# Weight decoding without GpSimd's add, one fp32 matmul in place of a split pair, and a new order for block 0

## The chip, the cores and the metric

The kernel runs on one core of a Trainium2 chip. A core has TensorE (PE), with its weight loads listed apart as PEld, VectorE (DVE), ScalarE (ACT), GpSimd (POOL) and SyncE (SP), which issues the transfers. The metric is the device time of one execution in microseconds (us), the median of several runs.

## The reference

Three stages follow one another, all in float32 (shapes in the comments).

```python
# 1. local + global attention, 4 batches x 8 heads, 512 local and 32 global positions, head size 64
out_g = softmax(scale * q_g @ k_all.T) @ v_all
out_l = softmax(concat([scale * q_l @ k_g.T, banded(scale * q_l @ k_l.T)])) @ v_all   # band of +-32
x = concat([out_g, out_l]) as (2176 tokens, 512)
# 2. soft mixture of experts, 8 experts x 4 slots
logits = x @ phi;  d = softmax(logits, over tokens);  c = softmax(logits, over slots)
slot_out[e] = relu((d.T @ x)[e] @ w1[e]) @ w2[e]
x = c @ slot_out
# 3. gated feed-forward layer, w_in 512 x 2048, w_out 2048 x 512
h = x @ w_in
out = (h * cos(h)) @ w_out
```

The last layer's weights reach the kernel as 64-bit words (`w_in` and `w_out` seen as int64, which are float64 numbers), so each weight is two 32-bit words, and the kernel makes a float32 of them itself. That is what is called decoding here.

## The kernel before

**Stages.** Attention runs in 40 units (32 with one pair of heads and one half of the positions each, 8 for the global rows), software-pipelined: for every step `s` a string of letters (`ORDER`, with exceptions in `TURN_OF`) names the stages in the order in which they are issued, each for another unit. Then come the experts, and then the feed-forward layer in four blocks of 512 tokens plus one tile of 128 (the global rows). In each block 16 slices `f` of 128 hidden columns are computed: `u_mm` (L1006, h of one slice), `u_round`, `u_frac`, `u_cos`, `u_mul` (the gate: L1012 on ACT, L1019 on DVE, L1026 on ACT, L1031 on DVE), a split into a high part (`u_hi` L1037 on ACT or `u_hi2` L1045 on DVE) and a rest (`u_lo`, L1050), and `o_pass` (L1117), twelve matmuls of 512 columns per slice in three passes of four: high x high, high x low, low x high.

**Order.** Nothing reorders the program: each engine works through its instructions as they are issued, and waits at the first that is not ready. In block 0 the order is the string `SWEEP`, one letter per step; I call the time of this string the sweep. After it, blocks 1 to 3 follow a fixed loop.

**What decoding takes.** For a tile of 128 x 512 weights, `high` (L156, ACT) makes the upper bits from the high word; another ACT instruction (L699 for `w_in`, L972 in `d_low` for `w_out`) makes the bits that come from the low word, a whole number; `shift3` (L151, DVE) shifts the upper bits left by three; `add_low` (L160, POOL) adds the two. `w_in` (16 tiles) is decoded during attention: stage `A` issues the two ACT instructions at the end of a step of the list `DEC`, stage `B` of the next step the shift, stage `C` the add. `w_out` (16 tiles, `f`) is decoded in the sweep, by the letters h, l, s, a. There each tile is then split for the matmul into a rounded high half (`d_h`: letter d on ACT L987, D on DVE L989) and a rest (`d_l`: letter e on DVE, E on POOL, both L993).

**w_in's part.** Before the sweep's slices can start, `w_in` is multiplied with the slot outputs: `cm_mm` (L925, letter 3, four times), then `cm_copy` (L932, letter 4, ACT) and `cm_rest` (L936, letter 8, DVE) split the result into two rounded parts, and `cm_sel` (L943, letter 5) sums the four groups of rows with two matmuls against a 0/1 matrix `sel_r`. The letters 0, 1, 2 do the same for the first 128 columns by a short way, 6 and 7 (L952, L957) split the sum for `u_mm`.

**The tile of global rows** has its own steps in the sweep: M (`x_mm` L1063), n, F, x, U, y or Y, z or Z (L1068 to L1090) and X (`x_out` L1096, three matmuls for each f).

**Buffers that make engines wait for each other.** `u_mm` writes into two PSUM banks in turn, so slice i+2 cannot start before the last reader of slice i (`u_mul` or `u_hi2`) is done. Upper bits, low bits and the joined `w_out` tile have three buffers each (`NC`), those of `w_in` one each, so the next `high` on ACT waits until the tile before is joined.

## Time and profile before

| | us |
|---|---|
| median of 3 runs | 404.56 (403.65 to 406.88) |
| span of the profiled execution | 401.8 |
| PE busy | 381.6 (95% of the span) |
| DVE busy | 274.7 (68%) |
| ACT busy | 226.3 (56%) |
| POOL busy | 211.9 (53%) |

The span runs from the first to the last instruction of one profiled execution; the page gives no other time of that execution, and the median of the runs shown is 2.8 us above this span. In the rows below, a line number is that of the kernel before, "x" a count, "idle before" the time for which the engine stood still ahead of the group, and the name behind `<-` what ended it.

### The profile page before, as it was taken

What the parts mean: (1) busy time and instruction counts of PE and PEld (TensorE: products, weight loads), DVE (VectorE), ACT (ScalarE), POOL (GpSimd) and SP (SyncE); (2) the same over time, 40 slices, a digit from 0 to 9 for tenths busy, and PEclk for the clock granted to TensorE, in tenths of its full rate; (3) what the DMA queues carried; (4) which work ended last, traced back from release to release, by engine and by line L of the source; (5) the groups of instructions that cost most, each with busy time, mean ns of one, the idle gap of its engine ahead of it and who ended that gap; (6) DMA issues with size and microseconds to landing.
All of it is one profiled execution on the core that took longest, in us unless ns stands there. A gap on an engine that the chain in (4) does not pass through costs nothing.

```text
span 401.8 us, 10160 instructions
## 1 busy us (share of the span) xinstructions
PE 381.6 (95%) x3922; PEld 287.2 (71%) x3922; DVE 274.7 (68%) x793; ACT 226.3 (56%) x462; POOL 211.9 (53%) x265
## 2 busy tenths in 40 slices
PE   7998989988989899999999899999999999999996
PEld 6777867766767543335677677888888888888885
DVE  5699788779859632138999988655556565665561
ACT  3488788778878313359888764433433433533430
POOL 0879879858862000026989796234434434354441
PEclk9999999999999999999999999999999999999999
DMA  7999999976859899999100000300002000110002
GB/s 260 366 364 409 406 411 409 403 264 249 285 181 342 310 374 409 409 408 409 75 0 0 2 0 1 132 1 1 2 0 106 0 1 2 44 60 2 0 0 106
DMA packets 23519, 72.36 MB, mean 180 GB/s; under 512 B 3120, under 2 KB 3888, under 8 KB 23472
## 3 DMA queue, kind: packets, MB, share of 16 engines
q1 hardware_dynamic: 23472, 71.72, 47.1%
...
## 4 chain that ended last, share of the span: by engine, by line
PE 76%; ACT 9%; DVE 7%; DMA 4%; issue 3%; SPq 1%; POOL 0%; DVEq 0%; ACTq 0%; POOLq 0%
PE bank L1117 38%; PE bank L306 6%; PE bank L861 4%; PE bank L826 4%; PE bank L351 3%; PE bank L1006 3%; PE bank L324 3%; DMA big<-in_w_out 3%; PE bank L419 2%; PE bank L451 2%; PE bank L443 2%; ACT sml L330 2%; PE bank L1096 2%; DMA big<-in_kq 2%; ACT sml L434 1%
## 5 line engine op out<-in xcount | busy, mean ns | idle before, releaser
L1050 POOL TENSOR_TENSOR big<-sml,sml 128x512 fp32r<-128x512 f32 x58 | 76.7, 1323 | 83.8 <-DVE sml L1039 73.3
L1117 PE MATMUL bank<-big,sml 128*128 128x512 f32 (+1 forms) x442 | 109.6, 382 | 0.4 <-DVE big L993 0.4
L1117 PEld LDWEIGHTS bank<-big,sml 128*128 128x128 f32 x442 | 81.2, 189 | 18.3 <-DVE big L993 0.9
L1012 ACT ACTIVATE sml<-bank 128x512 int32<-128x512 f32 x63 | 37.6, 596 | 87.7 <-PE bank L1006 87.5
L160 POOL TENSOR_TENSOR sml<-sml,sml 128x512 int32<-128x512 int32 x32 | 43.7, 1366 | 57.6 <-ACT sml L972 50.8
L1117 PE MATMUL bank<-big,big 128*128 128x512 f32 (+1 forms) x221 | 59.5, 381 | 0.0
L133 POOL TENSOR_SCALAR sml<-wide 64x258 f32<-64x258 f32 (+2 forms) x94 | 48.1, 511 | 15.1 <-PE bank L351 4.4
L1117 PEld LDWEIGHTS bank<-big,big 128*128 128x128 f32 x221 | 40.9, 188 | 8.6
L306 PEld LDWEIGHTS bank<-big,sml 128*64 128x64 f32 x672 | 34.8, 140 | 8.8 <-issue 5.4
L1019 DVE SCALAR_TENSOR_TENSOR sml<-sml,bank 128x512 f32<-128x512 int32 x32 | 21.9, 684 | 26.6 <-ACT sml L1012 26.6
L1019 DVE SCALAR_TENSOR_TENSOR wide<-sml,bank 128x512 f32<-128x512 int32 x32 | 22.0, 686 | 26.2 <-ACT sml L1012 26.0
L306 PE MATMUL bank<-big,sml 128*64 128x128 f32 (+2 forms) x672 | 38.7, 262 | 1.0 <-issue 1.0
L316 DVE CUSTOM_DVE_ANT_0 sml<-bank,mk 128x128 f32<-128x128 f32 x128 | 29.4, 286 | 8.4 <-PE bank L306 8.1
L133 POOL TENSOR_SCALAR sml<-big 64x32 f32<-64x32 f32 (+1 forms) x62 | 23.6, 381 | 14.8 <-PE bank L306 5.8
L318 DVE TENSOR_TENSOR sml<-sml,mx 128x512 f32<-128x512 f32 x32 | 26.7, 835 | 1.1
L1006 PE MATMUL bank<-big,sml 96*128 96x512 f32 x60 | 24.3, 405 | 1.5 <-DVE sml L1045 1.5
L351 PE MATMUL bank<-sml,sml 128*32 128x65 f32 x640 | 21.4, 223 | 4.1 <-ACT sml L330 3.4
L1117 PE MATMUL bank<-wide,sml 128*128 128x512 f32 (+1 forms) x102 | 24.8, 383 | 0.2 <-ACT sml L1037 0.2
L330 ACT ACTIVATE sml<-bank 128x512 f32<-128x512 f32 x32 | 18.9, 591 | 9.6 <-PE bank L324 9.3
L151 DVE TENSOR_SCALAR sml<-sml 128x512 int32<-128x512 int32 x32 | 22.3, 698 | 2.0 <-ACT sml L156 2.0
L1039 DVE CAST sml<-sml 128x512 fp32r<-128x512 f32 x46 | 20.3, 441 | 4.6
L1026 ACT ACTIVATE sml<-wide 128x512 f32<-128x512 f32 x32 | 20.0, 625 | 5.3 <-DVE wide L1019 5.3
...
## 6 DMA issues: line engine op xcount, KB each, us to landing
...
```

What stands on the lines that cost most here:

```text
L133: pool.tensor_scalar(out=out, in0=in_, scalar1=1.0, scalar2=0.0, op0=ALU.mult, op1=ALU.add)
L160: add.tensor_tensor(out=out.bitcast(I32), in0=ci, in1=r.bitcast(I32), op=ALU.add)
L306: pe.matmul(o, lhs, rhs, start=True, stop=True)
L316: dve.tensor_tensor_reduce(out=ss[:, g], in0=s[:, g], in1=mk[:, MASK[4 * key[3] + g]], op0=ALU.add, op1=ALU.max, scale=1.0, scalar=-3.0e38 ...
L318: dve.tensor_tensor(out=ss, in0=ss, in1=mx.to_broadcast([128, 4, 128]), op=ALU.subtract)
L330: act.activation(out=pt, in_=TT.pop(key), func=AF.Exp, scale=SCALE)
L351: pe.matmul(o[32 * qd:32 * qd + 32, i2, 65 * h:65 * h + 65], pt[:, c8 // 2, l0:l0 + 32], vt[:, HD * h:HD * h + HD + 1], start=True, stop=True)
L1006: pe.matmul(UU[s][:, 0:n], wcs[f], ctb[bi][0:96, 0:n].bitcast(F32R), start=True, stop=True)
L1012: act.activation(out=AA[s][:, 0:n], in_=UU[s][:, 0:n], func=AF.Copy, bias=0.25)
L1019: dve.scalar_tensor_tensor(out=FR[s][:, 0:n], in0=AA.pop(s)[:, 0:n], scalar=0.25, in1=UU[s][:, 0:n], op0=ALU.subtract, op1=ALU.subtract)
L1050: eng.tensor_tensor(out=gl[:, 0:n], in0=GG.pop(s)[:, 0:n], in1=GH[s][:, 0:n].bitcast(F32), op=ALU.subtract)
L1117: pe.matmul(acc[j][:, 0:c1 - c0], g, whl[f][k == 1][:, c0:c1], start=(f == 0 and k == 0), stop=(f == NFF - 1 and k == 2))
```

## The change

Both words are now joined by one VectorE instruction: ACT's instruction for the low word is scaled and offset so that its whole number lies within three bits, and `join` shifts the upper bits and ORs the low ones in. `shift3`, `add_low` and stage `C` of the attention's order go away, and with them letter s; letter a is now the join on DVE. `cm_sel` is a single matmul on unrounded float32 numbers, so `cm_rest` (letter 8) and the rounded copy of the 0/1 matrix go away. The string `SWEEP` is new. It does the same work with 16 letters s and 4 letters 8 less, and also moves some work between engines: d on ACT 14 to 7, D on DVE 2 to 9, E on POOL 13 to 6, e on DVE 3 to 10, u_hi on ACT (g) 8 to 13, u_hi2 on DVE (G) 10 to 5, v on POOL 12 to 11, V on DVE 6 to 7, R on DVE 1 to 0 and r on ACT 18 to 19, Y on DVE 2 to 1 and y on ACT 2 to 3.

```diff
-    def shift3(c):
-        ci = c.bitcast(I32)
-        dve.tensor_scalar(out=ci, in0=ci, scalar1=3, scalar2=None, op0=ALU.logical_shift_left)
-    def add_low(c, r, out, add):
-        ci = c.bitcast(I32)
-        add.tensor_tensor(out=out.bitcast(I32), in0=ci, in1=r.bitcast(I32), op=ALU.add)
+    def low(raw, r):
+        act.activation(out=r.bitcast(I32), in_=words(raw)[0].bitcast(U32), func=AF.Copy, scale=0.9 * 2.0 ** -29, bias=0.29)
+
+    def join(c, r, out):
+        dve.scalar_tensor_tensor(out=out.bitcast(I32), in0=c.bitcast(I32), scalar=3, in1=r.bitcast(I32),
+                                 op0=ALU.logical_shift_left, op1=ALU.bitwise_or)
...
-            act.activation(out=r.bitcast(I32), in_=words(raw)[0].bitcast(U32), func=AF.Copy, scale=2.0 ** -29)
+            low(raw, r)
...
             dc, n, raw, c, r = dpend.popleft()
-            shift3(c)
-            dadd.append((dc, n, c, r))
+            wi[dc, n] = smalls.popleft()
+            join(c, r, wi[dc, n])
...
-    def dec_c():
-        if dadd:
-            dc, n, c, r = dadd.popleft()
-            wi[dc, n] = smalls.popleft()
-            add_low(c, r, wi[dc, n], pool)
...
-        act.activation(out=p1s[n][1][:, c:512].bitcast(F32R), in_=o[:, c:512], func=AF.Copy)
-
-    def cm_rest(n):
-        (o, h, l), c = p1s[n], c0_of(n)
-        dve.tensor_tensor(out=l[:, c:512].bitcast(F32R), in0=o[:, c:512], in1=h[:, c:512], op=ALU.subtract)
+        act.activation(out=t[:, c:512], in_=o[:, c:512], func=AF.Copy)
...
-        for k, t in enumerate((h, l)):
-            pe.matmul(o[0:96, c:512], sel_r, t[:, c:512].bitcast(F32R), start=(k == 0), stop=(k == 1))
-            smalls.append(t)
+        pe.matmul(o[0:96, c:512], sel3, t[:, c:512], start=True, stop=True)
...
-    "h0lsh13ls2m43hraas8hfl4d5836c7434uEm5M8arm8gfvAr6cfhdBCsuE7cgulsm5rvgAfdvancBlmr6euGCFdAfBmx7aDC5Uch6uGyAEsM"
+    "0ll3h1al342Dmh5era34f65d7c3e6ulmM7rGn4fmvhAFcaxCrudBUgfElmVAcrBuhlfCgacYmvAdurBegzhfmClVcAruhCagaBdflm4AecDMVr"
```

**DVE, the start of the sweep.** These are DVE's first instructions in the sweep before (L151 the shifts, L957 letters 2 and 7, L936 letter 8, L1019 the first u_frac, L1031 the first u_mul):

```order
L151 TENSOR_SCALAR sml_2990<-sml_2990 128x512
L151 TENSOR_SCALAR sml_2991<-sml_2991 128x512
L957 SCALAR_TENSOR_TENSOR big_3037<-bank_74,big_3037 32x128
L151 TENSOR_SCALAR sml_2992<-sml_2992 128x512
L936 TENSOR_TENSOR sml_3048<-bank_75,sml_3047 128x384
L1019 SCALAR_TENSOR_TENSOR sml_3001<-sml_2999,bank_71 128x512
L936 TENSOR_TENSOR sml_3064<-bank_76,sml_3063 128x512
L957 SCALAR_TENSOR_TENSOR sml_3075<-bank_77,sml_3075 32x384
L1031 TENSOR_TENSOR sml_3005<-bank_71,big_3003 128x512
```

And now (L155 the join, L939 letters 2 and 7, L968 letter D, L972 letter e, L998 u_frac, L1010 u_mul, L1024 u_hi2):

```order
L155 SCALAR_TENSOR_TENSOR sml_2979<-sml_2973,sml_2976 128x512
L939 SCALAR_TENSOR_TENSOR sml_3023<-bank_74,sml_3023 32x128
L968 CAST big_3034<-sml_2979 128x512
L972 TENSOR_TENSOR big_3034<-sml_2979,big_3034 128x512
L155 SCALAR_TENSOR_TENSOR sml_2980<-sml_2974,sml_2977 128x512
L998 SCALAR_TENSOR_TENSOR sml_2984<-sml_2982,bank_71 128x512
L939 SCALAR_TENSOR_TENSOR sml_3049<-bank_77,sml_3049 32x384
L972 TENSOR_TENSOR wide_3052<-sml_2980,wide_3052 128x512
L1010 TENSOR_TENSOR sml_2988<-bank_71,big_2986 128x512
```

The three shifts and the two L936 ahead of the first u_mul are gone; two joins, a cast and two subtractions stand there instead.

**POOL, the start of the sweep.** Before, with L160 the add, L993 letter E and L1050 u_lo:

```order
L160 TENSOR_TENSOR sml_2996<-sml_2990,sml_2993 128x512
L160 TENSOR_TENSOR sml_2997<-sml_2991,sml_2994 128x512
L993 TENSOR_TENSOR wide_3066<-sml_2996,wide_3066 128x512
L160 TENSOR_TENSOR sml_2998<-sml_2992,sml_2995 128x512
L1050 TENSOR_TENSOR big_3010<-sml_3005,sml_3007 128x512
L993 TENSOR_TENSOR big_3116<-sml_2997,big_3116 128x512
L1050 TENSOR_TENSOR big_3011<-sml_3006,sml_3008 128x512
```

And now (L1029 u_lo, L972 letter E, L1069 letter z):

```order
L1029 TENSOR_TENSOR big_2993<-sml_2988,sml_2990 128x512
L972 TENSOR_TENSOR big_3094<-sml_2981,big_3094 128x512
L1029 TENSOR_TENSOR big_2995<-sml_2988,sml_2992 128x512
L1069 TENSOR_TENSOR big_3001<-big_2999,big_3000 128x512
L972 TENSOR_TENSOR big_3187<-sml_2981,big_3187 128x512
```

POOL has 43 instructions in the sweep before, and 19 now; the adds are gone, in attention (16) too.

## Rows read from the trace of the kernel before

**Rows 1.** Busy time by stretch: attention, experts, sweep, blocks 1 to 3 (columns: PE, PEld, DVE, ACT, POOL).

```profile
10.00:142.00 132.00, 122.11 (x2551) 95.88 (x2551) 107.61 (x505) 98.51 (x228) 91.51 (x169) 1.00 0.90 339
142.00:177.40 35.40, 35.30 (x303) 12.77 (x302) 8.46 (x23) 11.27 (x23) 0.00 (x0) 1.00 1.02 399
177.40:253.60 76.20, 71.55 (x340) 52.77 (x341) 69.32 (x99) 58.87 (x109) 60.00 (x43) 1.00 0.22 85
253.60:401.80 148.20, 144.64 (x669) 119.08 (x668) 83.95 (x146) 54.62 (x98) 59.52 (x46) 1.00 0.08 30
```

**Rows 2.** Chain that ended last, two pieces of block 3 (start us, length us, what).

```profile
347.52 2.79 PE bank L1117 x12
350.54 2.81 PE bank L1117 x15
```

**Rows 3.** Waits of PE in the sweep, the longest (us, times, longest).

```profile
PE bank L1006 <- DVE sml L1045: 1.5, 2, 0.8
```

**Rows 4.** Timeline of DVE, the `u_hi2` of slice 7, for which slice 9 waited.

```profile
212.23 0.67 DVE L1045 TENSOR_TENSOR sml<-bank,sml 128x512 fp32r<-128x512 f32 x1
```

**Rows 5.** Timeline of DVE, five instructions in a row (start, length, operation).

```profile
201.62 1.33 DVE L151 TENSOR_SCALAR sml<-sml 128x512 int32<-128x512 int32 x1
202.88 0.67 DVE L1019 SCALAR_TENSOR_TENSOR sml<-sml,bank 128x512 f32<-128x512 int32 x1
203.47 0.68 DVE L1031 TENSOR_TENSOR sml<-bank,sml 128x512 f32<-128x512 f32 x1
204.08 0.41 DVE L151 TENSOR_SCALAR sml<-sml 128x512 int32<-128x512 int32 x1
204.41 0.67 DVE L1072 SCALAR_TENSOR_TENSOR big<-big,bank 128x512 f32<-128x512 int32 x1
```

**Rows 6.** Timeline of POOL, the instruction that ran while that first shift began.

```profile
201.38 1.29 POOL L1050 TENSOR_TENSOR big<-sml,sml 128x512 fp32r<-128x512 f32 x1
```

**Rows 7.** Groups of DVE's instructions in the sweep (busy us, mean ns, idle before).

```profile
L151 DVE TENSOR_SCALAR sml<-sml 128x512 int32<-128x512 int32 x16 | 13.2, 827 | 1.2 <-ACT sml L156 1.2
...
L1050 DVE TENSOR_TENSOR big<-sml,sml 128x512 fp32r<-128x512 f32 x6 | 5.7, 958 | 0.1
L993 DVE TENSOR_TENSOR big<-sml,big 128x512 fp32r<-128x512 f32 x3 | 4.5, 1505 | 0.4 <-ACT big L987 0.4
...
L1090 DVE TENSOR_TENSOR big<-big,big 128x512 fp32r<-128x512 f32 x2 | 3.0, 1504 | 0.0
...
L989 DVE CAST big<-sml 128x512 fp32r<-128x512 f32 x2 | 2.3, 1150 | 0.0
```

**Rows 8.** The adds among POOL's groups in the sweep.

```profile
L160 POOL TENSOR_TENSOR sml<-sml,sml 128x512 int32<-128x512 int32 x16 | 22.8, 1426 | 52.2 <-ACT sml L972 50.8 <-DVE sml L151 1.4
```

**Rows 9.** Two lines over the whole run (duration ns min/median/max, first and last start).

```profile
L318 DVE TENSOR_TENSOR sml<-sml,mx x32: 691/706/1553, 7.5 to 126.5; 128x512 f32<-128x512 f32 x32
...
L1039 DVE CAST sml<-sml x46: 426/427/1051, 256.1 to 390.3; 128x512 fp32r<-128x512 f32 x46
```

**Rows 10.** Timeline at the sweep's start: DVE's second shift, and PE's first pass of slice 0.

```profile
178.38 1.17 DVE L151 TENSOR_SCALAR sml<-sml 128x512 int32<-128x512 int32 x1 [0.65 <-ACT sml L156]
...
186.09 2.13 PE L1117 MATMUL bank<-wide,sml 128*128 128x512 f32 x8 [0.25 <-ACT sml L1037]
```

**Rows 11.** Chain that ended last, one piece in the expert stage.

```profile
142.21 7.00 PE bank L826 x64
```

**Rows 12.** PE's groups in the sweep by form, the one of cm_sel.

```profile
L943 PE MATMUL bank<-sml,big 128*96 128x512 f32 x6 | 2.0, 408 | 0.5 <-DVE sml L957 0.5
```

**Rows 13.** Waits of weight loads for POOL in attention.

```profile
PEld bank L306 <- POOL sml L133: 2.6, 7, 0.8
```

**Rows 14.** Timeline of DVE, one shift in attention.

```profile
50.30 0.58 DVE L151 TENSOR_SCALAR sml<-sml 128x512 int32<-128x512 int32 x1 [0.84 <-ACT sml L156]
```

**Rows 15.** Groups of DVE's instructions from 10 to 142 us.

```profile
L318 DVE TENSOR_TENSOR sml<-sml,mx 128x512 f32<-128x512 f32 x30 | 25.3, 845 | 1.0
...
L151 DVE TENSOR_SCALAR sml<-sml 128x512 int32<-128x512 int32 x16 | 9.1, 569 | 0.8 <-ACT sml L156 0.8
```

More of the change, by code (lines that the diff above doesn't have):

```diff
@@ L628, in fused_kernel @@
     wid = deque((dc, n) for n in range(4) for dc in range(4))
-    dpend, dadd = deque(), deque()
+    dpend = deque()
     post = deque()
@@ L720, in pump @@
             key, n = wq[0][0], len(wq)
-            load_w(1, spare=1 + len(wid) + len(dpend) + len(dadd))
+            load_w(1, spare=1 + len(wid) + len(dpend))
             if len(wq) == n:
@@ L741, in fused_kernel @@
         "q": lambda s: prep_in(s + 3),
-        "C": lambda s: dec_c(),
         "m": lambda s: prep(s + 1, 1),
@@ L760, in fused_kernel @@
             STAGES[stage](s)
-        if dc_r and not wid and not dpend and not dadd:
+        if dc_r and not wid and not dpend:
             smalls.extend(dc_r.release() + dr_r.release())
@@ L894, in fused_kernel @@
     route_t(1, x_r())
-    sel_r = ctb[4][:, 128:224].bitcast(F32R)
-    dve.tensor_copy(out=sel_r, in_=sel3)
     ex_w2(0, lambda: ex_t(1), MID[0])
@@ L971, in d_low, with d_join @@
         DC[f, 1] = t = r_r()
-        act.activation(out=t.bitcast(I32), in_=words(wt["wo", f])[0].bitcast(U32), func=AF.Copy, scale=2.0 ** -29)
-    def d_shift(f):
-        shift3(DC[f, 0])
-    def d_add(f, eng):
+        low(wt["wo", f], t)
+    def d_join(f):
         DW[f] = wd_r()
-        add_low(DC.pop((f, 0)), DC.pop((f, 1)), DW[f], eng)
+        join(DC.pop((f, 0)), DC.pop((f, 1)), DW[f])
         bigs.append(wt.pop(("wo", f)))
@@ L1174, in fused_kernel @@
     kinds = {
-        "h": (d_hi, None), "l": (d_low, None), "s": (d_shift, None),
-        "a": (d_add, pool), "d": (d_h, act), "D": (d_h, dve), "e": (d_l, dve), "E": (d_l, pool),
+        "h": (d_hi, None), "l": (d_low, None), "a": (d_join, None), "d": (d_h, act), "D": (d_h, dve), "e": (d_l, dve), "E": (d_l, pool),
         "0": (lambda n: cm_dir(), None), "1": (lambda n: cm_hi("d"), None), "2": (lambda n: cm_lo("d"), None),
-        "3": (cm_mm, None), "4": (cm_copy, None), "8": (cm_rest, None), "5": (cm_sel, None), "6": (cm_hi, None), "7": (cm_lo, None),
+        "3": (cm_mm, None), "4": (cm_copy, None), "5": (cm_sel, None), "6": (cm_hi, None), "7": (cm_lo, None),
         "m": (u_mm, None), "r": (u_round, act), "R": (u_round, dve), "f": (u_frac, None), "c": (u_cos, None),
```

14 lines of the change are left out of this document (7 added, 7 removed).

## The prediction, made before the changed kernel ran

> **What bounds the kernel now.** I read the busy time by stretch first [rows 1], to see which stage has room. In blocks 1 to 3 the chain of work shows PE without a hole: two pieces start 3.02 us apart for 13 matmuls of 512 columns, 0.232 us each [rows 2]. No weight is decoded there, so that stretch stays. The experts (142 to 177.4) have PE busy for 35.30 of 35.40 us and stay too. What can move is the sweep, 76.2 us, and attention.
>
> What PE has to do in the sweep, by the program: 180 + 12 matmuls of `o_pass`, 48 of X, 19 `u_mm` and 8 of `cm_sel`, 267 x 0.232 = 61.9 us. The float32 work beside it: four groups of four side-by-side matmuls go at 7.00 us / 16 = 0.44 us a group [rows 11], so `cm_mm` is 1.8; the short way and the small x_mm matmuls are some 3.0 more, taken at that rate for their columns. Together 66.7 us in a window of 76.2, which ends where block 1's first pass begins: **9.5 us of PE's time are lost in the sweep**, and that is all that the sweep can give. The first pass of slice 0 starts at 186.09 [rows 10], 8.7 us after the sweep's start, with 5.0 us of work ahead of it (the short way, `cm_mm`, two sums, three `u_mm`, one x_mm): 3.7 us are lost at the start, 5.8 later.
>
> Who is late then? The list of PE's waits says DVE; the largest is `u_mm` waiting for `u_hi2`, 1.5 us in two waits [rows 3]. The timeline of DVE shows why: a shift takes 1.33 us where the one shortly after takes 0.41 [rows 5], and the long one began while POOL's u_lo (201.38 to 202.67) ran [rows 6]. Free instructions follow one another every 0.60 us (202.88, 203.47, 204.08), and a free shift holds DVE for 0.33 us (204.08 to 204.41) [rows 5]. The blocked time is the mean over the free duration in the five groups that are stretched [rows 7]: L151 16 x (0.827 - 0.41) = 6.7; L1050, L993, L1090 at 0.69 when free [rows 9] 6 x 0.27 = 1.6, 3 x 0.81 = 2.4, 2 x 0.81 = 1.6; L989 at 0.43 [rows 9] 2 x 0.72 = 1.4. Together **13.7 us on 29 instructions** (two Z's are among L1090, and six v, three e, two D, 16 shifts), while POOL is busy 60.0 of 76.2 us, 79% [rows 1].
>
> **The change, part by part.**
>
> *POOL.* Sixteen adds leave the sweep (22.8 us [rows 8]), and seven E and one v go to DVE: 43 instructions become 19, at the 1.29 us of a free one [rows 6] 24.5 us, a third of some 73.
>
> *DVE in the sweep.* Before, the work free of blocking is 16 shifts x 0.33 + 2 casts x 0.35 + 77 others x 0.60 = 52.2. After: a join has two inputs in SBUF and no row of before shows it. Nearest is L318, two inputs from SBUF, 0.69 free [rows 9], spaced 0.61; the lower bound is the shift's 0.33, the upper one L318's blocked 1.55. I take 0.61, since the join is read and written like L318. The change is then +16 x 0.28 = 4.5, seven casts +2.5, seven e +4.3, one V +0.6, less five G, four L936, one R and one Y, 11 x 0.60 = 6.6: **+5.3 us, 57.5**. The instructions that POOL can block become 44 (16 joins, 9 D, 10 e, 7 V, 2 Z). Each lost 13.7 / 29 = 0.47 us when POOL was 79% busy; at 34% that is 0.20, together 9 us (bounds: 0, if they never meet, and 13.7 as before). So DVE's load is 66 us before and after. What changes is where it lies.
>
> *Where it lies.* I count DVE's and PE's work up to the two places where `u_mm` waited 1.5 us. At slice 9 (needs G7 of before, u7 now): before, 25.0 us of DVE work, done at 212.9 [rows 4], so 10.5 us of blocking and waiting since 177.4. Now it is also 25.4 us, but 18 blockable instructions lose 3.7, and I follow the first slices by hand (ACT now has two low words ahead of the first high one, and each gate's cosine stands behind a decode) and find 3.4 us in which DVE waits for ACT: ready at 209.9. PE arrives after 27.3 us of work and the loss at its start, 177.4 + 27.3 + 3.5 = 208.2, so it waits 1.7. At slice 13, 40.4 of DVE work, 31 blockable instructions 6.4, and 3.4: 227.6; PE 177.4 + 43.6 + 3.5 + 1.7 = 226.2, wait 1.4. Between slices 9 and 10 the new order puts eight X in a row, 24 matmuls or 5.6 us of PE, which those counts include, and after slice 13 DVE gets ahead; at slice 18 nobody waits: DVE 177.4 + 56.5 + 9.0 + 3.4 = 246.3, PE 246.9. The 3.5 at the start: the shift of 1.17 us at 178.38 [rows 10] and two `cm_rest` no longer stand ahead of the first gate, so slice 0 starts near 185.0 instead of 186.09; its second pass needs `u_lo`, which POOL can only begin when slice 0's high part is there, and that and slice 1's high part give back 0.9. Lost in all 3.5 + 1.7 + 1.4 = 6.6 instead of 9.5: **-2.9 us**.
>
> *The sum's single matmul.* A pair of rounded matmuls costs 2 x 0.232 = 0.46; lone ones take 0.408 from start to end [rows 12]. A float32 one of 512 columns I take at the 0.44 of a group [rows 11]: nothing gained on PE; with the group read as four matmuls in a row the lower bound would be 0.11, and the upper is 0.88, twice the group. The work that goes is `cm_rest`'s, counted above. The Trainium skill, in "FP8 and Floating Point Precision" (section TensorE Precision Notes), speaks against this edit: it says that a true float32 matmul takes four passes through the array. By that the four sums would cost 4 x (4 x 0.232 - 0.46) = 1.9 us more and the sweep would give 1.0 instead of 2.9. The group's 0.44 us for 512 columns, 1.9 times 0.232, is against it, if four side-by-side matmuls do run at once.
>
> *Attention.* DVE pays 16 joins at 0.61 plus a block instead of 0.569 shifts [rows 15], some +0.2 each, 3 us; L318, stretched by 30 x (0.845 - 0.69) = 4.7 [rows 15], gets a third of that back. The join waits for ACT's low word too, where the shift waited only for the high one: at 50.30 [rows 14] it would start 0.5 later, with `f_local` and the next unit's maximum queued behind it. DVE is busy 107.6 of 132 us [rows 1], so that idle time hides most: +0.5 (bounds 0 and +3). POOL loses 16 adds, and weight loads waited 2.6 us for its copies [rows 13]; much of that lies beside the matmul ahead: -1.0 (bounds 0 and -2.6). Net **-0.5**. SP's order does not change, and `w_out` is not fetched later.
>
> Sum: -2.9 - 0.5 = **-3.4**, a span of 398.4, and with the 2.8 us between span and median, 404.56 - 3.4 = **401.2**.
>
> **The rivals.**
>
> *A larger gain.* The two engines hardly meet any more, since POOL's 19 come late and singly: blocking 0 to 4 instead of 9, no wait at slices 9 and 13, -6.0 in the sweep; with attention -1.0, 397.6. For it: every wait of PE in the list is for DVE. Against: 44 instructions can be blocked now, not 29.
>
> *No gain.* DVE's 57.5 us fill the window, and each wait taken away returns at another slice, or joins stop attention (+3): 403 to 405. For it: DVE's load is the same 66 us.
>
> *Four passes.* If a float32 matmul costs four of the rounded ones, 1.9 us more stand on PE before slice 6: 403.1. The Trainium skill's page above is the one that says so. Against it: [rows 11].
>
> *Slower.* The join is slow: an integer shift and OR at half the rate of L318, 1.2 us instead of 0.61. DVE then has 9.4 us more in the sweep, all of it ahead of PE, and 9 in attention, half hidden: 401.2 + 9.4 + 4.5 = 415. It decides from a join of about 0.75 (0.14 x 16 = 2.2 in the sweep, 1 in attention, against the 3.4). For it: no row shows this instruction. Against: the free shift of the same integers ran at 0.41.
>
> **How the numbers follow.** Forecast (400 to 403) 0.42, larger gain 0.28, no gain 0.17, four passes 0.04, slower 0.09. The range leaves out a little of both ends: 397.6 (no blocking at all) to 405.0 (no gain, or a join of 0.8). About 1%, 4.05 us, is what a measurement of this kernel can tell from no change, so faster means under 400.5: nearly all of the larger gain and a quarter of the forecast, 0.38; slower, over 408.6, only with a slow join, 0.07; the rest, 0.55, is within 1%.
>
> **What would show it.** Joins at 0.69 when free, and a mean under 0.95 in the sweep; POOL's busy time down by 35 us in the sweep and by 21 in attention; the pass of slice 0 near 185; block 1 starting near 250.7 instead of 253.6; PE's waits still for DVE, near slices 9 and 13; `cm_sel` at some 0.6 from start to end, like other lone float32 matmuls; the first slice of block 1 onward unchanged. It is wrong if the sweep's length moves by less than 1 or more than 6 us, or if attention's end moves by more than 2.

## The result, and the profile after

The changed kernel takes **400.7 us** (median, 399.55 to 401.0), the kernel before 405.09 in the same comparison: a ratio of 0.9898, with a 95% interval of 0.9872 to 0.9924. The prediction said 401.2, within 1% of before as the likeliest, and the result lies on that line: 1.0% faster, 0.8 to 1.3. The profiled execution has a span of 398.9 us, before 401.8; predicted was 398.4. The span fell by 2.9 us and the median by 4.4, because the execution profiled here was the longest of four, and that of before, by its span, the shortest.

| | before | after | predicted |
|---|---|---|---|
| median, us | 405.09 | 400.7 | 401.2 |
| span of the profiled execution | 401.8 | 398.9 | 398.4 |
| attention ends at | 142.14 | 142.75 | 0.5 earlier |
| experts | 35.31 | 35.74 | the same |
| sweep | 75.97 | 72.36 | 2.9 less |
| of it up to slice 0's first pass | 8.64 | 8.80 | 1.1 less |
| of it the rest | 67.33 | 63.55 | 1.8 less |
| POOL busy in the sweep | 60.0 | 26.8 | 35 less |
| DVE's time lost to blocking in the sweep | 13.9 | 6.7 | 9 |

Here, as in the expectations below, attention ends with the first matmul of the experts, and the sweep runs from the first matmul of the short way to the `u_mm` of slice 19, the first behind the string's own nineteen. The prediction used other ends for the sweep (76.2 us before), which shifts nothing in the differences. From that matmul to the last one every kernel here takes 144.53 or 144.54 us.

Busy time by stretch of the kernel after: attention, experts, sweep, blocks 1 to 3, with PE, PEld, DVE, ACT, POOL as in [rows 1].

```profile
10.00:142.70 132.70, 122.25 (x2551) 95.88 (x2551) 108.45 (x506) 97.89 (x227) 73.39 (x153) 1.00 0.89 338
142.70:178.40 35.70, 35.63 (x303) 12.62 (x301) 8.12 (x20) 11.23 (x23) 0.00 (x0) 1.00 1.02 398
178.40:250.80 72.40, 71.30 (x339) 53.36 (x340) 67.25 (x103) 58.33 (x109) 26.80 (x19) 1.00 0.23 90
250.80:398.90 148.10, 144.86 (x670) 119.24 (x668) 84.08 (x146) 54.53 (x98) 59.45 (x46) 1.00 0.08 29
```

The third row is the change: POOL's 19 instructions keep it busy for 37% of the sweep, not 79%, and the sweep is 3.6 us shorter. DVE is busy for 67.3 us of the sweep and stands idle for 5.1 (before: 69.1 and 6.9), and PE's busy time is the whole stretch less 1.1 us.

DVE's groups in the sweep after, the ones that POOL can block (busy us, mean ns, idle before), to be held against [rows 7].

```profile
L155 DVE SCALAR_TENSOR_TENSOR sml<-sml,sml 128x512 int32<-128x512 int32 x16 | 11.8, 740 | 1.2 <-ACT sml L149 1.2
L1029 DVE TENSOR_TENSOR big<-sml,sml 128x512 fp32r<-128x512 f32 x7 | 7.0, 996 | 0.0
...
L972 DVE TENSOR_TENSOR big<-sml,big 128x512 fp32r<-128x512 f32 x7 | 5.5, 782 | 0.0
L968 DVE CAST big<-sml 128x512 fp32r<-128x512 f32 x7 | 4.2, 603 | 0.0
...
L1069 DVE TENSOR_TENSOR big<-big,big 128x512 fp32r<-128x512 f32 x2 | 2.1, 1050 | 0.2 <-ACT big L1064 0.2
...
L968 DVE CAST wide<-sml 128x512 fp32r<-128x512 f32 x2 | 1.8, 899 | 0.0
```

The joins (L155) hardly meet POOL: 740 ns in the mean, against 827 for shifts that take 410 when free. What is lost over the free duration in these six groups (free: 0.68 for a join, 0.69 for the other two-input forms, 0.43 for a cast) is 0.9 + 2.1 + 0.7 + 1.2 + 0.7 + 0.9 = 6.5 us, and 6.7 counted instruction by instruction; before, 13.9 in the same count.

The join over the whole run, and the single sum L925 (duration ns min/median/max, first and last start).

```profile
L155 DVE SCALAR_TENSOR_TENSOR sml<-sml,sml x32: 675/691/1328, 24.2 to 235.6; 128x512 int32<-128x512 int32 x32
```

```profile
L925 PE MATMUL bank<-sml,cst x8: 486/592/670, 181.5 to 210.5; 128*96 128x512 f32 x6, 128*96 128x384 f32 x2
```

The join costs what L318 costs [rows 9], 0.69 us. The second row shows something that the prediction had missed: the program has four of these sums, and the trace has **eight records**. A float32 matmul leaves two here.

Chain that ended last, pieces of the sweep after (start, length, what).

```profile
184.43 1.00 PE bank L912 x8
...
203.37 0.86 PE bank L925 x2
204.45 2.78 PE bank L1096 x12
...
229.39 0.69 DVE big L1069
...
246.10 0.61 DVE sml L1010
247.26 3.74 PE bank L1096 x16
```

One sum of 512 columns is 0.86 us where twelve rounded matmuls are 2.78, 0.232 each; a pair of rounded ones is 0.46. `cm_mm` (L912), four instructions, eight records, is 1.00. From 229.39 to 246.10 the chain is mostly DVE's; up to 225 us and after 246.7 it is mostly PE's.

Waits of PE from 170 to 254 us, the whole list (us, times, longest), against [rows 3].

```profile
PE bank L985 <- DVE sml L1024: 0.7, 1, 0.7
PE bank L985 <- DVE sml L1010: 0.2, 1, 0.2
```

The 0.7 is at the sweep's start, as the timeline there shows (L1024 is `u_hi2` of slice 0, L985 `u_mm`, L1029 `u_lo`, L1096 `o_pass`; start, length, operation, in brackets what was waited for).

```profile
186.20 0.69 DVE L1024 TENSOR_TENSOR sml<-bank,big 128x512 fp32r<-128x512 f32 x1
...
186.95 0.50 PE L985 MATMUL bank<-big,sml 96*128 96x512 f32 x1 [0.70 <-DVE sml L1024]
...
187.16 1.30 POOL L1029 TENSOR_TENSOR big<-sml,sml 128x512 fp32r<-128x512 f32 x1 [58.60 <-ACT big L1047]
187.28 1.09 PE L1096 MATMUL bank<-big,sml 128*128 128x512 f32 x4
...
188.51 1.19 PE L1096 MATMUL bank<-big,big 128*128 128x512 f32 x4
```

Slice 0's high part is there at 186.89; its first pass and slice 2's `u_mm` follow, and then the second pass waits for POOL's `u_lo` until 188.47. After this the list has 0.2 us for the rest of the sweep. Before, it has 3.3 us there, 3.0 of them for DVE: the waits of `u_mm` for `u_hi2`, 1.5 [rows 3], and next in size these (L1087 is letter Y, L957 letter 7, L993 letter e).

```profile
PE bank L1063 <- DVE big L1087: 0.6, 1, 0.6
PE bank L943 <- DVE sml L957: 0.5, 1, 0.5
PE bank L1117 <- DVE big L993: 0.4, 1, 0.4
```

**Where the time went.** With the float32 matmuls at the length that the chain shows, PE's work ahead of the first pass is, after, 0.96 (short way) + 3.5 (`cm_mm`: 1.50 + 0.99 + 1.00) + 1.75 (two sums) + 0.7 (three `u_mm`) + 0.5 (x_mm) = 7.4 us; before, about 6.6, each of the two sums being 0.4 shorter. Behind the first pass it is 256 x 0.232 = 59.4, 1.2 for three x_mm, and two sums, 1.7 or (pairs) 0.9: 62.3 after, 61.5 before. So PE lost 2.0 us at the start and 5.8 behind it before; after, 1.4 and 1.3. **The gain lies in the 5.8 us that PE lost behind the first pass, of which 1.3 are left, less 0.8 of longer sums.** Of the 5.8 the list of waits shows 3.3, nearly all for DVE. The working rests on mean lengths, so it is good to a few tenths.

### The profile page after: what moved, and what is told of

Same layout as the page of the kernel before. It is cut to its first block, busy times and chain, and to the rows that moved or that the text cites. A ratio compares the mean times of both kernels' runs of the same rounds, so it can differ in the third digit from the quotient of the medians.

```text
span 398.9 us, 10096 instructions
## 1 busy us (share of the span) xinstructions
PE 382.2 (96%) x3922; PEld 288.1 (72%) x3922; DVE 273.3 (68%) x796; ACT 225.4 (57%) x462; POOL 160.8 (40%) x225
## 2 busy tenths in 40 slices
DMA packets 23519, 72.36 MB, mean 181 GB/s; under 512 B 3120, under 2 KB 3888, under 8 KB 23472
## 4 chain that ended last, share of the span: by engine, by line
PE 80%; ACT 9%; DVE 5%; issue 2%; DMA 1%; SPq 1%; POOL 0%; POOLq 0%; ACTq 0%
PE bank L1096 41%; PE bank L302 6%; PE bank L850 4%; PE bank L985 4%; PE bank L815 4%; PE bank L347 3%; PE bank L320 3%; PE bank L415 2%; PE bank L447 2%; PE bank L439 2%; ACT sml L326 2%; ACT sml L430 1%; DMA big<-in_kq 1%; PE bank L1075 1%; PE bank L370 1%
## 5 line engine op out<-in xcount | busy, mean ns | idle before, releaser
L1029 POOL TENSOR_TENSOR big<-sml,sml 128x512 fp32r<-128x512 f32 x57 | 74.8, 1313 | 154.5 <-DVE sml L1018 75.1
L1096 PE MATMUL bank<-big,sml 128*128 128x512 f32 (+1 forms) x442 | 109.0, 381 | 0.0
L1096 PEld LDWEIGHTS bank<-big,sml 128*128 128x128 f32 x442 | 81.3, 189 | 18.1 <-issue 0.5
L132 POOL TENSOR_SCALAR sml<-wide 64x258 f32<-64x258 f32 (+2 forms) x94 | 52.9, 563 | 26.2 <-issue 13.2
L1096 PE MATMUL bank<-big,big 128*128 128x512 f32 (+1 forms) x221 | 59.7, 382 | 0.1
L1096 PEld LDWEIGHTS bank<-big,big 128*128 128x128 f32 x221 | 40.8, 188 | 9.1 <-POOL big L1029 0.6
L998 DVE SCALAR_TENSOR_TENSOR sml<-sml,bank 128x512 f32<-128x512 int32 x32 | 21.9, 686 | 26.6 <-ACT sml L991 26.5
L998 DVE SCALAR_TENSOR_TENSOR wide<-sml,bank 128x512 f32<-128x512 int32 x32 | 21.9, 685 | 25.0 <-ACT sml L991 24.9
L132 POOL TENSOR_SCALAR sml<-big 64x32 f32<-64x32 f32 (+1 forms) x62 | 21.4, 345 | 27.5 <-PE bank L302 11.8
L985 PE MATMUL bank<-big,sml 96*128 96x512 f32 x64 | 26.7, 417 | 0.9 <-DVE sml L1024 0.7
L155 DVE SCALAR_TENSOR_TENSOR sml<-sml,sml 128x512 int32<-128x512 int32 x32 | 25.0, 784 | 3.4 <-ACT sml L152 2.1
L314 DVE TENSOR_TENSOR sml<-sml,mx 128x512 f32<-128x512 f32 x32 | 24.0, 751 | 1.1
L1096 PE MATMUL bank<-wide,sml 128*128 128x512 f32 (+1 forms) x102 | 24.5, 382 | 0.0
L1010 DVE TENSOR_TENSOR sml<-bank,big 128x512 f32<-128x512 f32 x32 | 21.9, 684 | 0.2
```

Of the source, the lines that this page charges most:

```text
L132: pool.tensor_scalar(out=out, in0=in_, scalar1=1.0, scalar2=0.0, op0=ALU.mult, op1=ALU.add)
L155: dve.scalar_tensor_tensor(out=out.bitcast(I32), in0=c.bitcast(I32), scalar=3, in1=r.bitcast(I32), op0=ALU.logical_shift_left, op1=ALU.bit ...
L314: dve.tensor_tensor(out=ss, in0=ss, in1=mx.to_broadcast([128, 4, 128]), op=ALU.subtract)
L985: pe.matmul(UU[s][:, 0:n], wcs[f], ctb[bi][0:96, 0:n].bitcast(F32R), start=True, stop=True)
L998: dve.scalar_tensor_tensor(out=FR[s][:, 0:n], in0=AA.pop(s)[:, 0:n], scalar=0.25, in1=UU[s][:, 0:n], op0=ALU.subtract, op1=ALU.subtract)
L1029: eng.tensor_tensor(out=gl[:, 0:n], in0=GG.pop(s)[:, 0:n], in1=GH[s][:, 0:n].bitcast(F32), op=ALU.subtract)
```

## The experiments

Each ran beside the kernel before. The table has the marks of the profiled executions; "lost" is the rest of the sweep less PE's work in it, worked out as above, and "blocked" DVE's time lost to POOL in the sweep.

| | median | ratio to before, interval | first pass | rest | sweep | lost | blocked |
|---|---|---|---|---|---|---|---|
| before | 405.09 | 1 | 8.64 | 67.33 | 75.97 | 5.8 | 13.9 |
| after | 400.7 | 0.9898, 0.9872 to 0.9924 | 8.80 | 63.55 | 72.36 | 1.3 | 6.7 |
| e1_join_only | 406.05 | 1.0047, 1.003 to 1.0064 | 8.47 | 69.22 | 77.69 | 7.7 | 8.6 |
| e2_sum_only | 404.36 | 0.9999, 0.9984 to 1.0015 | 8.64 | 67.83 | 76.47 | 5.5 | 13.8 |
| e9_shift_add | 407.53 | 1.0077, 1.0056 to 1.0097 | 9.60 | 69.69 | 79.29 | 7.4 | 12.4 |
| e3_pair_back | 403.45 | 0.9978, 0.9957 to 0.9999 | 9.78 | 64.76 | 74.54 | 3.3 | 6.6 |
| e4_sum_rounded | 400.57 | 0.9914, 0.9885 to 0.9944 | 8.78 | 64.06 | 72.84 | 3.0 | 6.8 |
| e5_attention_old | 401.5 | 0.9925, 0.9898 to 0.9953 | 8.78 | 63.57 | 72.36 | 1.3 | |
| e6_join_twice | 410.1 | one execution | 9.72 | 73.86 | 83.58 | 11.6 | 8.8 |
| c1_start | 401.93 | 0.994, 0.9915 to 0.9966 | 7.26 | 65.89 | 73.15 | 2.1 | 7.1 |
| c3_late_off_dve | 399.16 | 0.9868, 0.9831 to 0.9905 | 8.81 | 63.13 | 71.94 | 0.8 | 6.3 |
| c4_start_late | 400.17 | 0.9904, 0.9871 to 0.9936 | 7.27 | 65.48 | 72.74 | 1.7 | |
| c5_start_late_pair | 401.23 | 0.9941, 0.9913 to 0.9969 | 7.26 | 66.39 | 73.66 | 3.4 | |
| e10_rounded_late | 399.78 | 0.9897, 0.9867 to 0.9927 | 8.78 | 62.53 | 71.31 | 1.5 | 6.0 |

(In c1, c4 and c5 the rest holds 1.5 us more of PE's work, one `cm_mm` and the x_mm, which "lost" takes into account.)

**The clock in three of these profiles.** In the profiled executions of e4, e6 and e9, and in no other, TensorE's granted clock was at its lower level (1.2 GHz, not 2.4) for a while just behind the start of slice 0's first pass. Stretches within it, with the granted clock as the third number from the end:

```profile
187.60:190.90 3.30, 3.30 (x9) 2.50 (x9) 3.30 (x7) 3.24 (x6) 1.92 (x2) 0.50 1.03 410
186.70:190.00 3.30, 3.30 (x9) 2.50 (x8) 3.27 (x6) 2.77 (x6) 1.28 (x2) 0.50 1.03 411
188.30:191.60 3.30, 3.30 (x10) 2.53 (x9) 3.02 (x6) 2.52 (x6) 2.24 (x2) 0.50 1.04 413
```

(e4, e6, e9.) Just before, PE had stood idle for 1.5 to 1.6 us, waiting for slice 0's `u_hi2`. In e10 it waited 1.6 us at the same place, and the clock stayed at the higher level, so the wait alone doesn't decide it. What it costs shows in PE's timeline: the first pass and the `u_mm` of slice 3 in e4, and that `u_mm` in the kernel after, whose first pass starts at 187.28.

```profile
187.42 1.81 PE L1098 MATMUL bank<-big,sml 128*128 128x512 f32 x4
...
191.77 0.39 PE L987 MATMUL bank<-big,sml 96*128 96x512 f32 x1
```

```profile
190.47 0.39 PE L985 MATMUL bank<-big,sml 96*128 96x512 f32 x1
```

It is 4.35 us from the one to the other in e4, 4.34 in e6 and e9, and 3.18 or 3.19 in after, c3 and e10. So up to 1.2 us of the rest, the sweep and the loss of e4, e6 and e9 belong to the clock and not to the edit.

### Which part gains: join, order, or single sum

**e1_join_only**: joins everywhere, but the old string (without its s) and the pair of rounded matmuls.

```diff
-    "0ll3h1al342Dmh5era34f65d7c3e6ulmM7rGn4..."
+    "h0lh13l2m43hraa8hfl4d5836c7434uEm5M8arm8..."
...
-        pe.matmul(o[0:96, c:512], sel3, t[:, c:512], start=True, stop=True)
+        for k, t in enumerate((h, l)):
+            pe.matmul(o[0:96, c:512], sel_r, t[:, c:512].bitcast(F32R), start=(k == 0), stop=(k == 1))
```

> The decoding alone: joins on VectorE at the places of letter a, no shift and no add, in attention and in the sweep; the old order and the pair of rounded matmuls for the sum stay. The sweep (from the first matmul of the short way to block 1's first pass) took 76.2 us before and 72.6 after. Theory A, blocking: with 16 adds gone from GpSimd VectorE loses some 6 us instead of 13.7 to blocking, against 4.5 us more of its own work, so TensorE's waits for VectorE shrink: sweep 73.5 to 75, kernel 402 to 403.5. Rival B, only the new order pays: sweep 75.7 to 76.7, kernel as before (404 to 406).

The sweep became longer, 77.69 us, outside the ranges of both theories, and the kernel slower by half a per cent. DVE's group of joins, PE's longest wait and ACT's wait for a join in e1:

```profile
L156 DVE SCALAR_TENSOR_TENSOR sml<-sml,sml 128x512 int32<-128x512 int32 x16 | 17.8, 1124 | 0.1
```

```profile
PE bank L993 <- DVE sml L1032: 2.7, 3, 1.2
...
ACT big L974 <- DVE sml L156: 3.4, 1, 3.4
```

In the old string a join stands where POOL's add stood, and E and v are still POOL's (27 instructions, 37.1 us busy). So joins run into POOL's instructions, 1124 ns in the mean instead of 740 and 7.1 of the 8.6 us that DVE loses; `u_hi2` (L1032), behind them, is late for PE, and ACT's d waits 3.4 us for one join. The sum of the blocked time is not what decides, though: it fell by 5.3 us against before, DVE's busy time is the same (68.8 us, before 69.1), and its idle time rose from 6.9 to 8.9.

**e9_shift_add**: the other half: the new string and the single sum, but in the sweep a join is a shift on DVE and an add on POOL again.

```diff
     def d_join(f):
...
-        join(DC.pop((f, 0)), DC.pop((f, 1)), DW[f])
+        shift3(DC[f, 0])
+        add_low(DC.pop((f, 0)), DC.pop((f, 1)), DW[f], pool)
```

> After, with the sweep's weights joined the old way: at each letter a VectorE shifts (0.33 us free) and GpSimd adds (16 more instructions, 35 in all); attention and everything else as in after. The sweep was 72.4 us in after, 76.0 before (first matmul of the short way to the first u_mm behind the 19 of the string); VectorE was busy 73.7 of it in after. Theory A, VectorE bounds the sweep and blocking is what the decode change takes away: 16 x 0.28 = 4.5 us less of its own work, but GpSimd busy for some 48 us instead of 27, so blocking grows from 6.7 to 12 or more, and a tile is ready 1.3 us later: sweep 73.5 to 76. Rival B, the order alone made the gain: sweep 71 to 73.

79.29 us for the sweep, up to 1.2 of it the clock's: the longest of those that keep the work, and beyond theory A's 73.5 to 76. POOL's two largest groups in e9, the whole sweep (DVE's busy time is the third after the length), and what the add (L161) delays, ACT's cast d (L976) and low word (L152), and behind the cast DVE's e (L982):

```profile
L161 POOL TENSOR_TENSOR sml<-sml,sml 128x512 int32<-128x512 int32 x16 | 21.5, 1346 | 66.1 <-DVE sml L156 63.1 <-ACT big L1015 2.4 <-PE bank L1106 0.5
L1039 POOL TENSOR_TENSOR big<-sml,sml 128x512 fp32r<-128x512 f32 x11 | 15.2, 1385 | 7.5 <-ACT sml L1026 3.9 <-DMA big<-in_w_out 3.6
```

```profile
178.60:257.90 79.30, 74.44 (x339) 54.15 (x340) 68.78 (x102) 59.22 (x109) 48.63 (x35) 0.98 0.21 83
```

```profile
ACT big L976 <- POOL sml L161: 3.1, 4, 1.1
ACT sml L152 <- POOL sml L161: 2.1, 3, 1.1
...
DVE big L982 <- ACT big L976: 2.2, 3, 1.2
```

With the adds back POOL is busy for 49.1 us, and it blocks the work that the new string has given to DVE: 12.4 us. But DVE has some 4.5 us less work of its own, so its busy time is only 1.5 us more than after (68.8, after 67.3). What grew is its idle time, from 5.1 to 10.5 us. The tile now comes by way of POOL: ACT waits 5.2 us for the add in these two groups (before, where the order was made for it, 0.4), and DVE in turn for ACT. So in this order the add costs more by the lateness of the tile than by blocking. Theory A had named both, and put them too low together.

The join, then, gains 5.7 to 6.9 us of sweep under the new order with the single sum (79.29 to 72.36, less what may be the clock's), and loses 1.7 under the old one (75.97 to 77.69); the new order with the single sum loses 2.1 to 3.3 with the old decoding. Neither part is a gain; together they are. The sign doesn't hang on the clock: the two executions of e9 with a mean granted clock of 0.999 and 1.0 took 406.92 and 407.15 us, the kernel before 404.18 beside it.

**e2_sum_only**: the kernel before with the single float32 sum and without letter 8.

```diff
...
-        for k, t in enumerate((h, l)):
-            pe.matmul(o[0:96, c:512], sel_r, t[:, c:512].bitcast(F32R), start=(k == 0), stop=(k == 1))
+        pe.matmul(o[0:96, c:512], sel3, t[:, c:512], start=True, stop=True)
```

> The single float32 matmul alone, with the shift, the add and the old order (letters 8 left out). Theory A: a float32 matmul of 512 columns takes 0.86 us (two records of 0.43 in the trace of after) against 0.46 for the pair, 1.6 us more of TensorE's work, but the four cm_rest (2.4 us of VectorE) go and the waits for VectorE shrink by as much: sweep 75.5 to 76.7. Rival B, the passes lie wholly on the path: sweep 77.5 to 78, kernel 406 to 407. Rival C, it costs nothing on TensorE, as the prediction had it: sweep 73.8 to 75.

No change in the time, 0.5 us more in the sweep, as theory A had it. Its sum is 0.86 us in the chain as well. In the old order the two sums behind the first pass, 0.8 us longer together, and the four instructions that DVE saves come out about even (5.5 us lost, before 5.8).

**e3_pair_back**: the new kernel with pair and letter 8 put back.

```diff
-    "0ll3h1al342Dmh5era34f65d7c3e6ulmM7rGn4fmvhAF..."
+    "0ll3h1al342Dmh85era34f685d7c3e6ulmM7rGn48fmvhAF..."
```

> After, with the pair of rounded matmuls and cm_rest for the sum (letter 8 ahead of the first two sums and behind the last two copies). Theory A, TensorE bounds the sweep now: its work falls by 1.6 us and VectorE's rises by 2.4, of which the early half stands ahead of the first gate: sweep 71.3 to 72.6. Rival B, VectorE has no room: sweep 73.5 to 75.

Here the single sum matters: without it the sweep is 74.54, 2.2 us longer. DVE's group for letter 8, and PE's two longest waits in e3:

```profile
L926 DVE TENSOR_TENSOR sml<-bank,sml 128x512 fp32r<-128x512 f32 (+1 forms) x4 | 2.6, 655 | 1.0 <-ACT sml L922 1.0
```

```profile
PE bank L993 <- DVE sml L1032: 1.1, 1, 1.1
PE bank L933 <- DVE sml L926: 0.8, 2, 0.6
```

The four instructions are 2.6 us of DVE, and the sum itself waits for two of them; of 2.2 us 1.0 are ahead of the first pass. PE had 1.6 us less to do and gained nothing by it. VectorE has no room for them, as theory B had it. The blocked time is that of the kernel after (6.6 us), and yet PE loses 3.3 us behind the first pass instead of 1.3. So the join and the new order together gain 1.4 us of sweep (75.97 to 74.54); the other 2.2 of the 3.6 come only with the single sum.

### Which engine bounds the new sweep

**e6_join_twice**: every join of the sweep is made twice, which is 16 more instructions on DVE and nothing elsewhere.

```diff
     def d_join(f):
+        join(DC[f, 0], DC[f, 1], DW[f])
         join(DC.pop((f, 0)), DC.pop((f, 1)), DW[f])
```

> After, with each of the sweep's 16 joins issued twice into the same tile (the second changes nothing in the result). VectorE has 16 x 0.60 = 9.7 us more, no other engine anything. Theory A, VectorE bounds the sweep from end to end: sweep 72.4 + 9 to 11 = 81.5 to 83.5. Rival B, TensorE bounds it and VectorE has room: 73 to 77.

The sweep takes 83.58 us, +11.2 for some 16 x 0.6 = 9.7 us of work and 2.1 us more of blocking; up to 1.2 of the 11.2 is the clock's. PE's longest waits in e6:

```profile
PE bank L986 <- DVE sml L1025: 3.9, 4, 1.6
PE bank L1076 <- DVE big L1070: 1.1, 1, 1.1
PE bank L1076 <- DVE sml L939: 0.9, 1, 0.9
```

Nearly all that is added to DVE arrives at PE, and all the long waits are for DVE: it has next to no slack left.

**e4_sum_rounded**: each sum is one *rounded* matmul; the low part of the sum is left out of the computation. PE has 2.5 us less work in the sweep, and nothing else moves there.

```diff
-        act.activation(out=t[:, c:512], in_=o[:, c:512], func=AF.Copy)
+        act.activation(out=t[:, c:512].bitcast(F32R), in_=o[:, c:512], func=AF.Copy)
...
-        pe.matmul(o[0:96, c:512], sel3, t[:, c:512], start=True, stop=True)
+        pe.matmul(o[0:96, c:512], sel_r, t[:, c:512].bitcast(F32R), start=True, stop=True)
```

> After, with the sum made by one rounded matmul on a rounded copy; the rest of the sum (its low part) is left out. TensorE's work falls by 4 x 0.63 = 2.5 us and no other engine has more or less. Theory A, TensorE bounds the whole sweep: sweep 70.0 to 70.6, kernel 398 to 398.6. Rival B, the end of the sweep is VectorE's (its chain runs from 229 to 246.7 in after): the 2.5 us come back as a wait ahead of slice 18 or 17, sweep 71.8 to 72.7.

The sweep is 72.84, but 1.2 us of it are the clock's. Without them it would be some 71.7 (an estimate: 72.84 less 4.35 - 3.18), 0.7 shorter than after. PE's whole list of waits in e4:

```profile
PE bank L987 <- DVE sml L1026: 1.6, 1, 1.6
PE bank L1077 <- DVE sml L941: 0.4, 1, 0.4
```

The wait for slice 0's `u_hi2` (L1026) grew from 0.7 to 1.6, and the first pass begins 8.78 us after the sweep's start as before: the first two sums lie beside the work of ACT and DVE on slice 0. The last two shorten PE by 1.2, of which some 0.7 arrive; 0.4 go into a wait for DVE's letter 7 (L941). So theory A, that PE's work bounds the whole sweep (70.0 to 70.6), fell: the longer float32 sums cost this kernel nothing ahead of the first pass and some 0.7 us behind it. e10 against c3, both with the clock at the higher level, says nearly the same, 0.6.

**c3_late_off_dve**: the reverse: from tile 9 on, five casts go from DVE to ACT and four subtractions from DVE to POOL, which have room there. (The expectation speaks of six subtractions; the edit has four.)

```diff
-    "...XlenXhaXhGXlfXhacXDlaXhuXlemgVCrvDdmAhrECfecAfBuc"
+    "...XlenXhaXhGXlfXhacXdlaXhuXlEmgVCrvddmAhrECfEcAfBuc"
-    "GCumaArFlBGxfhmAUcarByVdBZuXDgXfEeXcXvmaCrVAfucCagMumvnCDrAgfmeBcFrCuxGAUmDByfErZcvBV..."
+    "GCumaArFlBGxfhmAUcarByVdBZuXdgXfEEXcXvmaCrVAfucCagMumvnCdrAgfmEBcFrCuxGAUmdByfErZcvBV..."
```

> After, with five late casts (D) moved to ScalarE and six late subtractions (e) to GpSimd, at the same places of the string, from weight tile 9 on. VectorE's own work falls by 5 x 0.35 + 6 x 0.61 = 5.4 us, GpSimd's rises by 7.8 to 35 us, ScalarE's by 2.6. Theory A, VectorE's chain ends the sweep (from 229 to 246.7 in after): sweep 70 to 71.5, kernel 398.5 to 399.8. Rival B, GpSimd's longer hold blocks VectorE as much as is taken off, or ScalarE is late: sweep 72 to 74.

DVE's instructions of the sweep take 68.5 us instead of 73.7, and the sweep is 0.4 shorter, 71.94, just between the ranges of the two theories. DVE's longest wait from 187 to 251 us, and PE's one wait from 179 to 262 us:

```profile
DVE wide L998 <- ACT sml L991: 3.5, 3, 1.5
...
PE bank L985 <- DVE sml L1024: 0.7, 1, 0.7
```

DVE now waits for ACT, and behind the first pass PE waits for nobody; 0.8 us are lost there. So PE is the next limit, at once. The median is the lowest of all, 399.16, but its interval overlaps that of the kernel after, and most of the difference of 1.5 us lies in stages that the edit doesn't touch: it isn't shown to be faster.

**e10_rounded_late**: e4 and c3 together, to take the load off both (the low part of the sum is left out here too).

> The one rounded matmul of e4_sum_rounded (the low part of the sum is left out, 2.5 us less on TensorE) and the late casts and subtractions off VectorE of c3_late_off_dve (4 us less there) together. Alone, the first left the sweep at 72.8, the second at 71.9, after has 72.4. Theory A, in after TensorE and VectorE bound the sweep to within half a microsecond of each other, so that relieving one shows the other: relieving both gives 69.3 to 70.3. Rival B, a third thing bounds it (ScalarE with 72 us of busy time, or the chain of one slice from u_mm to u_mul): 71.2 to 72.0.

71.31 us, 1.1 less than after and 0.6 less than c3: in the range of rival B, less of a gain than theory A had expected. The first pass still begins at 8.78, PE's two waits are those of e4, and 1.5 us are lost behind it. So relieving PE brings something once DVE is relieved, and the start is a third limit that neither edit touches.

### The start, and attention

**c1_start**: the first 59 letters stand in another order, so that slice 0 is ready earlier.

```diff
-    "0ll3h1al342Dmh5era34f65d7c3e6ulmM7rGn4fmvhAFcaxCrudBUgfElmVAcr..."
+    "0ll3h1al342Dmrh5efa367cm4ur4G5dfmvAc6eMluC73ngFrBhafxUdVElmAcr..."
```

> After, with the first 63 letters of the string in another order: round of slice 0 ahead of the second high word, the second cast and subtraction and the second w_in part behind the first gate, the last cm_mm behind the first pass. No work is added or taken away. TensorE's first pass starts 8.8 us after the sweep's start in after. Theory A, what bounds the sweep is VectorE's queue from the start on: an earlier first gate takes 1 to 1.7 us off the start (7.1 to 7.8), and most of it comes back as a wait later: sweep 71.5 to 72.5. Rival B, the start is lost time of all engines: sweep 70.5 to 71.3.

The first pass begins at 7.26 instead of 8.80, and the sweep is 73.15, longer by 0.8 and above both ranges. PE's two longest waits in c1 are for letters 2 and 7 (L939):

```profile
PE bank L985 <- DVE sml L939: 0.7, 1, 0.7
PE bank L912 <- DVE sml L939: 0.6, 1, 0.6
```

One `cm_mm` (1.0) and the x_mm (0.5) were moved behind the first pass, so it is earlier by just what no longer stands ahead of it; that work comes back later, with 0.8 us of new losses. Theory A, that the earlier start is given back, held, and more than that was given back. **c4_start_late** joins this start to c3's moves:

> Both edits to the string: the other start (first pass 1.5 us earlier, sweep 73.15 alone) and five late casts on ScalarE and four late subtractions on GpSimd (sweep 71.94 alone). Theory A, in after VectorE and TensorE are within half a microsecond of each other: with VectorE relieved by 4 us the earlier start is kept, sweep 70.2 to 71.0, kernel 397.3 to 398.3. Rival B, the earlier start comes back as waits for another engine (ScalarE, which has 72 us of busy time): sweep 71.7 to 72.5.

72.74, just above rival B's range: c3's 0.4 us on top of c1, and the earlier start is worth nothing with the relieved DVE either, so theory A of this run fell. **c5_start_late_pair** is c4 with the pair (and letter 8) for the last two sums:

```diff
...
+        if n > 1:
+            (_, h, l), c = p1s.pop(n), c0_of(n)
+            rs[n] = o = acc_free.popleft()
+            for k, t in enumerate((h, l)):
+                pe.matmul(o[0:96, c:512], sel_r, t[:, c:512].bitcast(F32R), start=(k == 0), stop=(k == 1))
```

> As c4_start_late, and the last two of the four sums made by the pair of rounded matmuls with cm_rest on VectorE again: TensorE's work falls by 2 x 0.40 = 0.8 us, VectorE's rises by 1.2. Theory A, with VectorE relieved TensorE bounds the sweep, so its work counts now: 0.4 to 0.8 us shorter than c4_start_late. Rival B, VectorE still bounds: 0.5 to 1.2 us longer.

73.66, 0.9 longer than c4, as rival B had it: two more instructions on DVE cost more than the 0.8 us that PE saves, even where DVE had been relieved later on.

**e5_attention_old**: the kernel after, with the old shift, add and stage `C` in attention only.

```diff
-ORDER = "abecdBrqmgpfA"
+ORDER = "abecdBrqmgpfCA"
...
-            join(c, r, wi[dc, n])
+            shift3(c)
+            dadd.append((dc, n, c, r))
```

> After, with w_in decoded in attention as before (shift on VectorE, add on GpSimd in stage C); the sweep is that of after. The first expert matmul started at 142.14 in before and 142.75 in after; in the other kernels of this study that have the joins in attention at 141.6 to 143.0, and in two with shift and add at 142.1 and 143.2. Theory A, attention does not feel the decode: 142.0 to 143.3, kernel 400.2 to 401.4. Rival B, the joins cost attention 0.6 us as the two single profiles read: 142.1, kernel 399.8 to 400.4. Rival C, GpSimd's relief had helped: 143.5 to 144, kernel over 401.7.

Sweep 72.36, equal to that of the kernel after, and 401.5 us with an interval that overlaps. Its attention ends at 143.55, in rival C's range (the time lies between A's and C's). Over all the profiles attention ends at 142.14, 143.22 and 143.55 in the three with the old decoding (before, e2, e5), and between 141.56 and 143.50 in those with joins. The means, 143.0 of three and 142.5 of eleven, differ by the 0.5 us that was predicted, but three profiles with a spread of 1.4 us can't show that; attention's share of the gain stays open.

## Why the prediction was right

The total is right and the place is right: the gain lies in the sweep, in waits of PE for DVE. That it comes from POOL no longer blocking DVE is shown only in part. The blocked time did fall by 7.2 us; but in e1 it fell by 5.3 and the sweep grew, in e3 it is that of the kernel after and the sweep is 2.2 longer, and e9 shows a second price of POOL's add, the lateness of the tile. What the runs show is that join, new order and single sum gain together; how much of it is blocking stays open. Step by step:

- **POOL's load.** 33 us less in the sweep (35 predicted), 18 less in attention (21 predicted). In attention the 94 wide ones of POOL's own copies became longer, 563 ns in the mean, 511 before (the 62 narrow ones shorter, 345 and 381); why isn't shown.

```profile
L132 POOL TENSOR_SCALAR sml<-wide 64x258 f32<-64x258 f32 (+2 forms) x94 | 52.9, 563 | 26.2 <-issue 13.2
```

- **The join** was taken at 0.61 spaced and 0.69 free, from L318 [rows 9], and is 0.675 to 0.69. The slow join, the rival on the other side, fell with that; a mean under 0.95 was named, and it is 0.740.
- **Blocking.** Predicted 9 us on 44 instructions, measured 6.7, so 0.15 us each where the proportion to POOL's busy share gave 0.20. Before it was 13.9 on 29, 0.48 each. That the blocked time falls although more instructions can be blocked was right, and e9 shows the condition: 44 instructions at nearly the same places, with POOL busy for 61% of the sweep, are blocked for 12.4 us, 0.28 each.
- **The waits at slices 9 and 13**, 1.7 + 1.4 us, did not occur; PE's later waits are 0.2 us by the list, 1.3 lost in all. This is the term that was mis-sized against the change: 3.1 forecast where 1.3 came. Up to slice 7's `u_mul` (L1010), which slice 9's `u_mm` (L985) needs, DVE lost 2.1 us to blocking (3.7 predicted) and 1.7 waiting for ACT (3.4 predicted). So it was done 30.4 us after the sweep's start and not 32.5, while PE came 32.1 us after it and not 30.8, kept back by the start and the longer sums:

```profile
208.23 0.68 DVE L1010 TENSOR_TENSOR sml<-bank,sml 128x512 f32<-128x512 f32 x1
```

```profile
210.54 0.80 PE L985 MATMUL bank<-big,sml 96*128 96x512 f32 x1
```

  At slice 13 it was the same: blocking 3.1 (6.4 predicted), ACT 2.4 (3.4), DVE done after 47.5 us and not 50.2, PE there after 48.7.
- **The start** was predicted 1.1 us earlier and is 0.2 later (8.80 against 8.64). The shift of 1.17 us [rows 10] and `cm_rest` are gone, though D and two e stand on DVE now, and slice 0's cosine does begin earlier, 5.3 us after the sweep's start, before 6.0; its `u_mul` gains 0.4 of that. But slice 0's high part has moved from ACT to DVE, where `u_hi2` stands behind letter 7 (L939), and is there 8.4 us after the start, before 8.6; and slice 2's `u_mm`, which must wait for it, now stands ahead of the first pass. The prediction's account of the start left these two out. That POOL's `u_lo` delays the second pass was right (188.51).
- **The single sum** was taken at 0.44 us and takes 0.86. The step that failed is the reading of [rows 11]: "x64" was taken for 64 matmuls, sixteen groups in 7.00 us. They are records, two to a float32 matmul, so 32 matmuls, eight groups, 0.875 each. The Trainium skill, "FP8 and Floating Point Precision" (TensorE Precision Notes), had the rule, four passes: an estimate of 4 x 0.232 = 0.93, and 0.86 was measured, so the trace agrees with it to within 8%. The rival *four passes* was right in its premise, then, and was given 0.04; but its price, 403.1, did not follow: the first two sums lie beside slice 0's gate, and of the 1.2 us by which e4 and e10 shorten the other two only 0.6 to 0.7 arrive. What they buy, four instructions less on a DVE that has no room, is 2.2 us (e3).
- **PE's loss in the sweep** was put at 9.5 us before; with float32 work at its real length it is 7.9, of which the start has 2.0 and not 3.7. So there was less to win, and a larger part was won.
- **Attention** was put at -0.5; the runs can't tell this from nothing.

In the sweep -2.9 was predicted, -0.2 of it net at the start and -2.7 behind it (5.8 to 3.1), and -3.6 was measured: the start gave +0.2, so 0.4 worse; two longer sums behind it 0.8 worse; the waits there 1.8 better (1.3 left and not 3.1). Two terms sized too well and one sized too badly left the total 0.6 off. That they nearly cancel is luck, and so is part of the median's agreement: the attention ended 0.6 later and not 0.5 earlier, the experts took 0.4 more, and between span and median lie 1.8 us here where 2.8 were assumed. *No gain*, whose reason was that DVE is as full as before, is near what e1 and e9 do, and they lose; what the prediction did not see is that the parts must come together.
